# Top-k attention ahead of a mixture-of-experts attention, one core: MAX8s between the two-input instructions of the second selection level, and a re-planned order of issue

## The chip, the core and the metric

The kernel runs on one core of a Trainium2 chip. A core has engines that run side by side, each with its own in-order queue: TensorE (PE; PEld is its weight load), VectorE (DVE), ScalarE (ACT), GpSimd (POOL), and SyncE (SP), which here issues the transfers. They meet in on-chip memory and wait for each other by semaphores. The metric is the device time of one execution in microseconds, less is better. Before the change the median of 3 runs is 1224.13 us (1223.06 to 1224.57).

## The reference

Two attentions follow each other, both over 8 batches of 576 rows. The first has 8 heads of 64 and keeps for each row only the scores that are at least the row's 32nd largest:

```python
scores = scale * np.matmul(q, k.transpose(0, 1, 3, 2))
kth = np.partition(scores, -top_k, axis=-1)[..., -top_k:-top_k + 1]
scores = np.where(scores >= kth, scores, -1000000000.0)
attn = np.exp(scores - np.max(scores, axis=-1, keepdims=True))
attn = attn / (np.sum(attn, axis=-1, keepdims=True) + 1e-09)
out = np.matmul(attn, v)
```

Its output, heads side by side (512 wide), is the input of the second, which has 4 experts. Each expert is a causal attention with its own projections of 64 columns. A gate, the softmax over the two largest of 4 logits a row, weighs the experts' outputs, and each expert's result goes through its own output projection:

```python
logits = x @ w_gate                      # two largest of 4, softmax over them
for e in range(E):
    a = causal_softmax(scale * (x @ wq[e]) @ (x @ wk[e]).T)
    out += (weight of e, 0 if not chosen) * (a @ (x @ wv[e]) @ wo[e])
```

## The kernel before

**Pairs and groups.** The heads go in 32 pairs (8 batches of 4). The rows of a pair make 9 tiles of 128 rows, `j` = 0 to 8; three tiles are a group, so there are 96 groups. For each group TensorE makes the scores (`scores`, slot<-opa or opb), ScalarE copies them to memory (`copy`, L541, tile s), and VectorE selects.

**The selection on VectorE**, all of it in `topk`. `f1` (L552) takes the maxima of the two halves of each row into `fa` (3 x 288 = 864 elements a partition), `f3` (L555) the minima into `fb`. `f4` is the second level: L560 writes the maxima of the halves of `fa` into `cand`, L561 the minima back into `fa`, L563 the maxima of the halves of those maxima into `oct`, L564 their minima into `cand`; these are 432, 432, 216 and 216 elements. All six are two-input instructions (TENSOR_TENSOR). `f6` (L572) then takes the eight largest of `fb` for each of the three tiles (MAX8 over 288), `f5` those of the two halves of `fa` (72 each), and `win` and `rep` find the 32 largest in four rounds of MAX8 and MATCH_REPLACE8.

**GpSimd beside it.** `mark` (L568) is a copy of one column of `oct`. It computes nothing that is used; it makes GpSimd's queue wait until the second level is that far, and `compare` (L612, a count of candidates that could be missed) and `sub` (L454, the low half of a later pair's operands) depend on it. `tails` (L580) copies three values of `cand`.

**After the selection.** `mask` on ScalarE turns the scores and the threshold into zeros and negative numbers, `stats` makes the row's maximum and the logarithm of its sum (its transposes are `s8`, L706), `st` makes the masked scores transposed (eight products, the last of them bf16 products with the mask, 64 to 128 columns), `exp` their exponentials (pt), `av` the products with v. After four pairs `moe` runs the second attention: `vproj` and `proj` (projections), `s_stage` (scores), `t_stage` (transposes, L1035 and L1039), `c4` (transposes of scales), `avm` (products with v), `prod` (output projection). All products with matmul go through one helper, so that they have one line, L274.

**What sets the order.** No scheduler of the compiler does. The kernel's own planner (`Plan`) is given tasks, each with an engine, a cost in ns written beside it, the tasks that it waits for, the buffers that it takes, and a due time in units of pairs (the `D_...` constants and, by kind of task, the table `BIAS`). `order` then plays the engines forward: each engine takes, of the tasks that could start within `SLACK` ns of the earliest, the one that is due first. The instructions are issued in that order. `PORT` names VectorE's tasks that the planner keeps apart from GpSimd's. The order is fixed when the program is built; at run time only semaphores decide when an instruction starts.

Of the kernel before, what the change touches and what calls it, by code (L numbers as in the profile page):

```python
# [17 lines left out]
S = 576  # L18
# [46 lines left out]
class Task:  # L65
    __slots__ = ("eng", "dur", "fn", "deps", "prio", "bufs", "lat", "n", "start", "end", "outs", "left", "tag")

    def __init__(self, eng, dur, fn, deps, prio, bufs, lat):
# [27 lines left out]

class Plan:
# [8 lines left out]
    SLACK = 46.592  # L106
# [16 lines left out]
    def add(self, eng, dur, fn, deps=(), prio=0.0, bufs=(), lat=0.0, tag=None):  # L123
# [3 lines left out]
        t = Task(eng, dur, fn, [d for d in deps if d is not None], prio, bufs, lat)  # L127
        t.n, t.tag = len(self.tasks), tag
        for b in t.bufs:
            b.users += 1  # L130
            self.rings.add(b.ring)
        self.tasks.append(t)
        return t

    def order(self):
        engs = {t.eng: [0.0, []] for t in self.tasks}
        port = {"DVE": 0.0, "POOL": 0.0}
# [36 lines left out]
        out = []  # L174
        clock = Clock()
        picks, stale = {}, set(engs)
        while len(out) < len(self.tasks):
# [9 lines left out]
            dur = clock.run(s, t.dur * PEF) if e == "PE" else t.dur  # L187
# [29 lines left out]
def dve(n):  # L217
    return (n + 66) / 0.96


def pool(n):
# [5 lines left out]
BIAS = {"<lambda>": 12.025746, "again": 6.983961, "av": 0.306567, "avm": 15.637129, "c1": 5.880716, "c2": -13.131783,  # L227
        "c3": -25.554085, "c4": 3.739867, "c5": -30.11967, "cast": 21.794626, "cast_swap": -12.929197, "check1":
        -12.521071, "check2": 41.941845, "check3": -32.989098, "compare": 12.828602, "constants": -4.616309,
        "copy": -7.533133, "count": 18.029105, "diag": 13.44438, "dup": -0.254198, "dup1": -19.40904, "dup2":  # L230
# [4 lines left out]
        "load_": -6.225866, "load_swap": -1.289504, "loadv": 6.903006, "low_again": -11.353865, "m_stage":  # L235
        -39.727842, "mark": 15.671427, "mask": -11.217948, "neg": 2.920136, "neg2": -12.787457, "o_stage":
# [3 lines left out]
        "st": -0.031636, "store": -10.105639, "sub": 9.813498, "t_stage": -4.44225, "tails": 2.712787, "vproj":  # L240
        1.088363, "win": 18.27658, "xh": 2.409038, "xl": 17.765869}
D_K2 = 26.942808
D_PREP = 4.978065
D_SC = 0.540315
D_TIE = 12.261253
D_MASK = 4.158611
D_STAT = -1.038851
D_TAIL = 0.276506
D_STEP = 0.103192
D_MOE = 4.217281  # L250
D_LAST = 4.050745
D_PEN = 3.97376
D_SPAN = 4.129727
# [5 lines left out]
def kernel(ctx, tc, qk, vL, wq, wk, wv, wo, out):  # L259
# [262 lines left out]
    def topk(w, general):  # L522
# [4 lines left out]
        for g in range(3):  # L527
# [5 lines left out]
            for n, j in enumerate(js):  # L533
# [9 lines left out]
                a = add("PE", 600 if j != 4 else 1150, scores, need, bufs=[sl, s3] + used(w, j), prio=0)  # L543
# [51 lines left out]
            t = add("DVE", 2 * dve(432) + 2 * dve(216), f4, [t], bufs=[fa, c, oc], prio=P0)  # L595
            marks.append(add("POOL", 200, mark, [t], bufs=[oc], prio=-9))
            compare_last()
            t = add("DVE", 3 * dve(288), f6, [t], bufs=[fb, c], prio=P0)
            t = add("DVE", 6 * dve(72) - 45, f5, [t], bufs=[fa, c], prio=P0)
            tl = add("POOL", 200, tails, [t], bufs=[c], prio=0)  # L600
            for r in range(4):
                n = 72 if r < 2 else 168
                t = add("DVE", 3 * dve(n), lambda r=r, win=win: win(r), [t], bufs=[oc, c, w.top], prio=P0, tag="win")
                if r < 3:
                    t = add("DVE", 3 * dve(n) + 165, lambda r=r, rep=rep: rep(r), [t], bufs=[oc, c, w.top], prio=P0, tag="rep")
# [51 lines left out]
    def stats(w, x):  # L657
# [57 lines left out]
        t2 = add("POOL", 420, s2, [t], bufs=b1, prio=0)  # L715
# [6 lines left out]
        t8 = add("PE", 54 * n + 130, s8, [t2, t7], bufs=[st, sl], prio=0)  # L722
        return add("ACT", act(S) + act(64) if x == 0 else act(512), s9, [t8],
# [3 lines left out]
    def tail(w, shift, xb):  # L727
# [39 lines left out]
        for j in STO:  # L767
# [11 lines left out]
            a = add("PE", 785 if j != 4 else 1520, lambda j=j, sl=sl: st(j, sl), need, bufs=[sl, pt] + used(w, j, True) + mb, prio=2, tag="st")  # L779
# [4 lines left out]
        for j in (0, 1, 2, 3, 4):  # L784
# [3 lines left out]
            a = add("PE", 1121 if j != 4 else 833, lambda j=j, pts=pts: av(j, pts), [es[k] for k in jj] + [w.v, a],  # L788
                    bufs=pts + [acc, w.vt], prio=1, tag="av")
# [6 lines left out]
        a = add("PE", 250, neg, [c], bufs=[acc, xb], prio=1)  # L796
# [5 lines left out]
        return [c, d, add("POOL", 460, dup, [c, d], bufs=[xb], prio=1)]  # L802


    def moe(b, p, xbs, xdone, wd, span, final):
# [41 lines left out]
        for t in range(5):  # L847
# [21 lines left out]
            a = add("PE", 1440, vproj, last + wd["v"], bufs=[sl, v2] + xbs, prio=3)  # L869
# [72 lines left out]
        for gp in range(2):  # L942
# [6 lines left out]
            for name, k in (("q", 0), ("k", 2)):  # L949
# [3 lines left out]
                for dt in range(4):  # L953
# [8 lines left out]
                    a = add("PE", 800, proj, last + wd[name] + [a], bufs=[sl, qk] + xbs, prio=3)  # L962
# [11 lines left out]
                a = add("PE", 250, neg, [c], bufs=[sl, qk], prio=3, tag="neg2")  # L974
                d = add("ACT", act(S), ev2, [a], bufs=[sl, qk], prio=3)
                ready += [c, d]
                if name == "q":
# [11 lines left out]
                    spread = add("POOL", 1120, diag, [c, d], bufs=[qk, bd], prio=3)  # L989
# [3 lines left out]
            for t in (0, 1, 2, 3, 4):  # L993
# [54 lines left out]
                pe = (720, 720, 935, 1106, 920)[t]  # L1048
                when(pe)
                a = add("PE", pe, s_stage, ready + [spread], bufs=[sl, pr, sm, qk, ptm, bd], prio=3)  # L1050
# [3 lines left out]
                pe = (225, 354, 560, 800, 760)[t]  # L1054
                when(pe)
                a = add("PE", pe, t_stage, [a], bufs=[s2, pr], prio=2)
# [33 lines left out]
            a = add("POOL", 206, c1, exps, bufs=[sm], prio=3)  # L1090
# [3 lines left out]
            a = add("PE", 750, c4, [a], bufs=[sm, sl], prio=3)  # L1094
# [16 lines left out]
            a1 = add("PE", 1534, lambda av=av: av((0, 1, 2)), pts + evs, bufs=[acc, ptm, v2], prio=3, tag="avm")  # L1111
            when(1900)
            a2 = add("PE", 1750, lambda av=av: av((3, 4)), [a1], bufs=[acc, ptm, v2], prio=3, tag="avm")
# [13 lines left out]
        for t in range(5):  # L1127
# [18 lines left out]
            a = add("PE", 1470, prod, split + wd["o"], bufs=[sl, oo, o], prio=3)  # L1146
# [107 lines left out]
```

## Time and profile before

| | us |
|---|---|
| median of 3 runs | 1224.13 |
| the profiled execution | 1221.66 |
| its span, first to last instruction | 1219.9 |
| TensorE busy | 1130.6 (93%) |
| VectorE busy | 1097.2 (90%) |
| ScalarE busy | 989.3 (81%) |
| GpSimd busy | 411.2 (34%) |

The profile is one execution. Its span leaves out what lies around the first and the last instruction, which makes the execution's time a little longer. Busy time is the union of an engine's records. Records of neighbouring instructions can overlap, since an instruction's record runs from its start to the landing of its last result; the distance between two starts is then what an instruction costs its engine. For TensorE the granted clock (PEclk) is shown as a share of full speed. A row that says `<-` after a time names what ended the wait.

### The profile page before, as it was taken

To read this page: it belongs to the slowest core of one execution; us is meant where nothing else is said; L and a number is where in the kernel's file an instruction comes from. 1 tells how busy PE (TensorE), PEld (TensorE's weight loads), DVE (VectorE), ACT (ScalarE), POOL (GpSimd) and SP (SyncE) were. 2 spreads that over 40 slices of the span, in tenths; PEclk is the share of its full clock that TensorE was granted. 3 is DMA by queue.
4 is the path that set the end of the run, shared out by engine and by line. 5 is a ranking of instruction groups with operands and counts; after the bars stand their busy time and mean duration, and the time that the engine had idled before them with its cause. 6 is when DMAs were issued, how large, how long until landed. Compare 5 with 4: busy or idle time off the path is not lost. (4 is left out here: it accounts for less than half of the span.)

```text
span 1219.9 us, 28284 instructions
## 1 busy us (share of the span) xinstructions
PE 1130.6 (93%) x9330; PEld 919.9 (75%) x9330; DVE 1097.2 (90%) x4745; ACT 989.3 (81%) x2050; POOL 411.2 (34%) x803
## 2 busy tenths in 40 slices
PE   3578799999999999999999999999999999999996
PEld 3456568887788777887788877887778877887785
DVE  7999999999999999999989999899999999899021
ACT  5677777889888887989788888988888898888554
POOL 4323223424325332253224333253333442242102
PEclk8698999999999999999999999999999999999999
DMA  7132323223332232233322233323322333220101
GB/s 198 43 89 68 102 75 86 55 67 105 111 89 66 72 110 71 81 90 96 107 80 69 56 105 104 90 66 90 104 72 67 90 107 111 65 71 15 46 2 42
DMA packets 45578, 98.56 MB, mean 81 GB/s; under 512 B 7792, under 2 KB 7792, under 8 KB 45424
## 3 DMA queue, kind: packets, MB, share of 16 engines
q1 hardware_dynamic: 45424, 96.67, 28.9%
q8 instruction: 76, 1.25, 0.4%
q14 instruction: 78, 0.64, 0.2%
HBM read 32.06 MB, written 9.44 MB: 34 GB/s over the span
## 5 line engine op out<-in xcount | busy, mean ns | idle before, releaser
L781 ACT ACTIVATE pt<-slot 128x576 f32<-128x576 f32 x288 | 185.9, 652 | 101.2 <-PE slot L274 99.3
L632 ACT ACTIVATE mask<-s,top 128x576 bf16<-128x576 f32 x288 | 215.6, 773 | 8.6 <-DVE top L585 7.9
L274 PE MATMUL slot<-opa,opa 128*128 128x256 f32 (+3 forms) x984 | 200.9, 328 | 21.4 <-ACT s L541 13.6
L274 PE MATMUL acc<-pt,vt 128*64 128x320 f32 (+3 forms) x1152 | 203.3, 422 | 3.9 <-ACT pt L781 3.9
L274 PEld LDWEIGHTS slot<-opa,opa 128*128 128x128 f32 (+1 forms) x984 | 146.1, 195 | 62.1 <-ACT s L541 26.2
L274 PE MATMUL slot<-opb,opb 128*128 128x320 f32 (+1 forms) x960 | 186.1, 314 | 4.3 <-DMA opb<-raw 3.2
L541 ACT ACTIVATE s<-slot 128x576 f32<-128x576 f32 x288 | 176.1, 651 | 5.7 <-PE slot L274 5.2
L568 POOL COPY scrap<-oct 128x1 f32<-128x1 f32 x96 | 35.6, 371 | 423.0 <-DVE oct L563 422.2
L274 PEld LDWEIGHTS slot<-opb,opb 128*128 128x128 f32 x960 | 141.3, 193 | 26.0 <-issue 18.9
L585 DVE MAX8 top<-cand 128x8 f32<-128x168 f32 x576 | 152.8, 320 | 0.0
L274 PEld LDWEIGHTS acc<-pt,vt 128*64 128x64 f32 (+1 forms) x1152 | 95.0, 143 | 51.0 <-ACT pt L781 16.0
L274 PE MATMUL slot<-negi,mask 128*128 128x128 bf16 (+3 forms) x1632 | 128.4, 217 | 0.0
L552 DVE TENSOR_TENSOR fa<-s 128x864 f32<-128x864 f32 x96 | 103.7, 1081 | 21.6 <-ACT s L541 21.6
L572 DVE MAX8 cand<-fb 128x8 f32<-128x288 f32 x288 | 112.5, 446 | 0.0
L612 POOL TENSOR_TENSOR ind<-cand,top 128x513 bf16<-128x513 f32 x96 | 100.3, 1045 | 6.4 <-ACT ind L620 6.4
L555 DVE TENSOR_TENSOR fb<-s 128x864 f32<-128x864 f32 x96 | 101.0, 1052 | 0.0
L274 PEld LDWEIGHTS <-mask 128*128 128x128 bf16 (+1 forms) x1632 | 79.0, 101 | 24.3 <-issue 5.2
L585 DVE MAX8 top<-oct 128x8 f32<-128x72 f32 x576 | 94.7, 220 | 0.0
L590 DVE MATCH_REPLACE8 cand<-top,cand 128x168 f32<-128x168 f32 x288 | 88.7, 318 | 0.0
L706 PE MATMUL slot<-identf,stat 128*4 128x128 f32 x288 | 43.6, 280 | 35.4 <-DVE stat L702 23.4
L620 ACT ACTIVATE ind<-ind,tiny 128x513 bf16<-128x513 bf16 (+1 forms) x96 | 69.8, 727 | 7.2 <-POOL ind L612 6.8
L274 PE MATMUL slot<-opb,k2b 128*128 128x320 f32 x320 | 70.6, 302 | 4.2 <-ACT opb L710 3.8
(192 smaller groups left out, 2507.6 us busy)
## 6 DMA issues: line engine op xcount, KB each, us to landing
raw<-in_qk_dram SPq DMA_DIRECT2D x31, 576.0 KB, 3.7
opb<-raw SPq DMA_DIRECT2D x93, 144.0 KB, 3.4
opa<-raw SPq DMA_DIRECT2D x93, 144.0 KB, 2.4
vt<-in_vL_dram SPq DMA_DIRECT2D x32, 320.0 KB, 3.4
opb<-opb SPq DMA_DIRECT2D x62, 144.0 KB, 2.4
opa<-opa SPq DMA_DIRECT2D x62, 144.0 KB, 2.4
out_dram<-pr SPq DMA_DIRECT2D x32, 256.0 KB, 2.2
k2a<-opa SPq DMA_DIRECT2D x32, 144.0 KB, 2.3
```

Source lines behind the costliest of these rows:

```text
L274: nc.tensor.matmul(o, l, r, start=start, stop=stop, skip_group_check=True)
L541: nc.scalar.activation(s3.t[:, n], sl.t[:, o0:o0 + S], AF.Copy)
L552: v.tensor_tensor(out=fa.t, in0=s3.t[:, :, 0:288], in1=s3.t[:, :, 288:576], op=OP.max)
L555: v.tensor_tensor(out=fb.t, in0=s3.t[:, :, 0:288], in1=s3.t[:, :, 288:576], op=OP.min)
L572: v.max(out=c.t[:, n, 160:168], in_=fb.t[:, n])
L585: v.max(out=w.top.t[0][:, j, 8 * r:8 * r + 8], in_=oc.t[:, n] if r < 2 else c.t[:, n, 0:168])
L590: v.match_replace(out=c.t[:, n, 0:72] if r == 1 else src, in_values=src, imm_value=LOW, in_to_replace=w.top.t[0][:, j, 8 * r:8 * r + 8])
L612: nc.gpsimd.tensor_tensor(out=ind.t[:, 0:513].rearrange("p (a n) -> p a n", a=3), in0=c.t, in1=m32[:, js[0]:js[0] + 3, 31:32].to_broadcast ...
L620: nc.scalar.activation(ind.t[:, 0:n], ind.t[:, 0:n], AF.Sign, bias=tiny, accum_out=signs[:, 3 * w.p + g:3 * w.p + g + 1])
L632: nc.scalar.activation(w.mask[j].t, s3.t[:, n], AF.Relu, bias=w.top.t[0][:, j, 31:32], scale=-1.0)
L706: nc.tensor.transpose(sl.t[0:4, j * P:(j + 1) * P], ft(parts()[2][:, j]), identf)
L781: es[j] = add("ACT", act(S), lambda sl=sl, pt=pt, o0=o0: nc.scalar.activation(pt.t, sl.t[:, o0:o0 + S], AF.Exp, scale=0.125), [a], bufs=[s ...
```

## The change

Two things change. In the second level the three MAX8 over `fb`, which stood behind the four two-input instructions, now stand one by one between them: first, MAX8, second, MAX8, third, MAX8, fourth. `mark` now copies a column of `cand` that the fourth writes, so that it waits for the fourth instead of the third. And the planner is given another account of the engines: tasks on TensorE have a kind (LONG, SHORT, MIXED, TURN), and one that begins long behind one that ended short is charged 107 ns; their costs are written anew; GpSimd's tasks other than the mark are started at least 160 ns behind VectorE's two-input work; the tables of due times have other numbers. The order of issue of all engines comes out differently.

```diff
+LONG, SHORT, EITHER, MIXED, TURN = 1, 2, 3, 4, 5
...
-    SLACK = 46.592
+    SLACK = 48.1507
+    GAP = 160.0
+    SWITCH = 107.0
...
                 if e == "POOL":
-                    s = max(s, port["DVE"])
+                    s = max(s, port["DVE"] + (0.0 if t.tag == "mark" else self.GAP))
...
-            dur = clock.run(s, t.dur * PEF) if e == "PE" else t.dur
+            dur = t.dur
+            if t.kind:
+                if short and t.kind not in (SHORT, TURN):
+                    dur += self.SWITCH
+                t.first = short
+                short = t.kind in (SHORT, MIXED) or t.kind == EITHER and not short
+            if e == "PE":
+                dur = clock.run(s, dur * PEF)
...
-D_MASK = 4.158611
+D_MASK = 1.607309
...
-            def f4(fa=fa, c=c, oc=oc):
+            def f4(fa=fa, fb=fb, c=c, oc=oc):
+                def low(n):
+                    v.max(out=c.t[:, n, 160:168], in_=fb.t[:, n])
                 l, r = fa.t[:, :, 0:144], fa.t[:, :, 144:288]
                 v.tensor_tensor(out=c.t[:, :, 0:144], in0=l, in1=r, op=OP.max)
+                low(0)
                 v.tensor_tensor(out=l, in0=l, in1=r, op=OP.min)
+                low(1)
                 l, r = c.t[:, :, 0:72], c.t[:, :, 72:144]
                 v.tensor_tensor(out=oc.t, in0=l, in1=r, op=OP.max)
+                low(2)
                 v.tensor_tensor(out=r, in0=l, in1=r, op=OP.min)
-            def mark(oc=oc, g=g):
-                nc.gpsimd.tensor_copy(scrap[:, g:g + 1], oc.t[:, 0, 0:1])
-            def f6(fb=fb, c=c):
-                for n in range(3):
-                    v.max(out=c.t[:, n, 160:168], in_=fb.t[:, n])
+            def mark(c=c, g=g):
+                nc.gpsimd.tensor_copy(scrap[:, g:g + 1], c.t[:, 0, 143:144])
...
-            t = add("DVE", 2 * dve(432) + 2 * dve(216), f4, [t], bufs=[fa, c, oc], prio=P0)
+            t = add("DVE", 2706, f4, [t], bufs=[fa, fb, c, oc], prio=P0)
...
-            a = add("PE", 785 if j != 4 else 1520, lambda j=j, sl=sl: st(j, sl), need, bufs=[sl, pt] + used(w, j, True) + mb, prio=2, tag="st")
+            a = add("PE", 767 if j != 4 else 1500, lambda j=j, sl=sl: st(j, sl), need, bufs=[sl, pt] + used(w, j, True) + mb, prio=2, tag="st",
+                    kind=MIXED)
```

What stands in VectorE's queue for one group before, in the middle of the program (`fa`, `fb`, `cand`, `oct` as above, `s` the copied scores, `top` the values found; what stands in brackets are the semaphores that the row waits for, DVE being its own):

```order
L552 TENSOR_TENSOR fa0_89<-s31_88 128x864 [waits Activation_49]
L555 TENSOR_TENSOR fb0_90<-s31_88 128x864
L560 TENSOR_TENSOR cand1_94<-fa0_89 128x3x144 [waits DVE_49]
L561 TENSOR_TENSOR fa0_89<-fa0_89 128x3x144 [waits DVE_49]
L563 TENSOR_TENSOR oct1_92<-cand1_94 128x216
L564 TENSOR_TENSOR cand1_94<-cand1_94 128x3x72 [waits DVE_49]
L572 MAX cand1_94<-fb0_90 128x8 x3
```

And after, for a group at about the same place:

```order
L569 TENSOR_TENSOR fa0_89<-s30_87 128x864 [waits Activation_49]
L572 TENSOR_TENSOR fb0_90<-s30_87 128x864
L579 TENSOR_TENSOR cand0_93<-fa0_89 128x3x144 [waits DVE_49]
L577 MAX cand0_93<-fb0_90 128x8 [waits DVE_49]
L581 TENSOR_TENSOR fa0_89<-fa0_89 128x3x144 [waits DVE_49]
L577 MAX cand0_93<-fb0_90 128x8
L584 TENSOR_TENSOR oct0_91<-cand0_93 128x216
L577 MAX cand0_93<-fb0_90 128x8
L586 TENSOR_TENSOR cand0_93<-cand0_93 128x3x72 [waits DVE_49]
```

The three MAX8 moved into the openings; the first of them has a wait that its forerunner did not need.

On TensorE, in the second attention of the fourth batch, the two transposes of the first block of rows (`identf,pr`) and what stands around them before (`opa_1,opa_0` rows are scores, `acc<-pt,vt` is `av`, the last row begins an `st`):

```order
L274 MATMUL slot_65<-opa_1_70,opa_2_71 128x320
L274 MATMUL acc_67<-pt_122,vt_86 128x256
L274 MATMUL acc_67<-pt_122,vt_86 128x320
L274 MATMUL slot_66<-opa_1_70,opa_0_69 128x256
L274 MATMUL slot_66<-opa_1_70,opa_0_69 128x320
L274 MATMUL slot_66<-opa_1_70,opa_2_71 128x256
L274 MATMUL slot_66<-opa_1_70,opa_2_71 128x320
L1035 MATMUL slot_64<-identf,pr_145 128x128 x2
L274 MATMUL slot_65<-opa_0_75,opa_1_76 128x256
```

And after (`qk,qk` is the end of an `s_stage`, the last row begins an `st`):

```order
L291 MATMUL slot_65<-qk_3_136,qk_0_133 128x256 x2
L291 MATMUL acc_67<-pt_120,vt_86 64x256
L291 MATMUL acc_67<-pt_122,vt_86 64x256
L291 MATMUL acc_67<-pt_122,vt_86 64x320
L291 MATMUL acc_67<-pt_120,vt_86 64x320
L1053 MATMUL slot_66<-identf,pr_145 128x128 x2
L291 MATMUL slot_64<-opb_0_78,opb_1_79 128x320
```

The transposes, which stood alone between scores and masked scores, now stand directly behind an `av`, and no scores lie between.

## Rows read from the trace of the kernel before

**Rows 1.** The page: busy us, share of the span, instructions of each engine.

```profile
PE 1130.6 (93%) x9330; PEld 919.9 (75%) x9330; DVE 1097.2 (90%) x4745; ACT 989.3 (81%) x2050; POOL 411.2 (34%) x803
```

**Rows 2.** Busy us by stage: stretch, length, engines, granted clock, DMA share, GB/s.

```profile
0.00:190.00 190.00, 131.82 (x875) 100.29 (x875) 179.05 (x788) 132.54 (x247) 64.61 (x121) 0.87 0.35 96
190.00:1128.00 938.00, 919.55 (x7773) 754.16 (x7772) 903.51 (x3922) 810.71 (x1700) 330.79 (x643) 1.00 0.30 83
1128.00:1219.90 91.90, 79.19 (x686) 65.47 (x684) 14.62 (x37) 46.04 (x105) 15.81 (x40) 0.98 0.09 31
```

**Rows 3.** VectorE's waits: total us, times, longest; 190 to 1128, then 0 to 190.

```profile
DVE fa L552 <- ACT s L541: 16.9, 19, 1.6
DVE v L867 <- ACT v L864: 6.5, 17, 0.8
...
DVE fa L552 <- ACT s L541: 4.7, 2, 4.4
```

**Rows 4.** TensorE's waits from 190 to 1128, the longest in total.

```profile
PE slot L706 <- DVE top L585: 5.4, 6, 1.1
```

**Rows 5.** VectorE's timeline, one undisturbed group: start, us, instruction, count.

```profile
90.89 1.05 DVE L555 TENSOR_TENSOR fb<-s 128x864 f32<-128x864 f32 x1
91.85 0.60 DVE L560 TENSOR_TENSOR cand<-fa 128x432 f32<-128x432 f32 x1
92.49 0.61 DVE L561 TENSOR_TENSOR fa<-fa 128x432 f32<-128x432 f32 x1
93.01 0.38 DVE L563 TENSOR_TENSOR oct<-cand 128x216 f32<-128x216 f32 x1
93.42 0.38 DVE L564 TENSOR_TENSOR cand<-cand 128x216 f32<-128x216 f32 x1
93.73 1.17 DVE L572 MAX8 cand<-fb 128x8 f32<-128x288 f32 x3
94.82 0.22 DVE L576 MAX8 cand<-fa 128x8 f32<-128x72 f32 x1
```

**Rows 6.** GpSimd's groups by form: count, busy us, mean ns, idle before and releaser.

```profile
L454 POOL TENSOR_TENSOR raw<-raw,opa 128x576 f32<-128x576 f32 x31 | 51.6, 1665 | 36.6 <-ACT opa L445 36.6
L454 POOL TENSOR_TENSOR raw<-raw,opb 128x576 f32<-128x576 f32 x31 | 44.2, 1426 | 43.9 <-ACT opb L445 37.3 <-DVE top L585 4.0 <-DVE oct L590 2.6
L568 POOL COPY scrap<-oct 128x1 f32<-128x1 f32 x96 | 35.6, 371 | 423.0 <-DVE oct L563 422.2 <-DVE oct L590 0.4
```

**Rows 7.** TensorE's timeline from 610 to 622 us.

```profile
610.20 0.95 PE L274 MATMUL slot<-x,wk 128*128 128x288 f32 x6
611.08 1.19 PE L274 MATMUL acc<-pt,vt 128*64 128x256 f32 x8
...
615.59 0.96 PE L274 MATMUL slot<-x,wk 128*128 128x288 f32 x6
616.38 1.23 PE L274 MATMUL slot<-opb,opb 128*128 128x320 f32 x8
...
620.39 1.04 PE L274 MATMUL slot<-x,wk 128*128 128x288 f32 x6
621.27 1.00 PE L274 MATMUL slot<-wv,x 128*128 128x260 f32 x7
```

**Rows 8.** VectorE's first selection instruction (L552) by stage: busy us and count.

```profile
190.00:1128.00 938.00, 85.33 (x79) 1.00 0.30 83
```

**Rows 9.** Timelines of GpSimd's subtraction, twice, and of VectorE beside the first.

```profile
398.03 2.93 POOL L454 TENSOR_TENSOR raw<-raw,opa 128x576 f32<-128x576 f32 x1 [1.64 <-ACT opa L445]
...
607.42 1.40 POOL L454 TENSOR_TENSOR raw<-raw,opa 128x576 f32<-128x576 f32 x1 [3.21 <-ACT opa L445]
...
399.72 1.71 DVE L561 TENSOR_TENSOR fa<-fa 128x432 f32<-128x432 f32 x1
```

**Rows 10.** VectorE's groups by form: the second instruction of the second level, mean ns.

```profile
L561 DVE TENSOR_TENSOR fa<-fa 128x432 f32<-128x432 f32 x96 | 64.0, 666 | 3.3
```

**Rows 11.** The same instruction in the view of its tile: shortest, median, longest ns.

```profile
L561 DVE TENSOR_TENSOR fa<-fa x96: 607/608/1705, 17.7 to 1120.4; 128x432 f32<-128x432 f32 x96
```

More of the change, by code (lines that the diff above doesn't have):

```diff
@@ L65, with __init__ @@
 class Task:
-    __slots__ = ("eng", "dur", "fn", "deps", "prio", "bufs", "lat", "n", "start", "end", "outs", "left", "tag")
-    def __init__(self, eng, dur, fn, deps, prio, bufs, lat):
+    __slots__ = ("eng", "dur", "fn", "deps", "prio", "bufs", "lat", "n", "start", "end", "outs", "left", "tag", "kind",
+                 "first")
+    def __init__(self, eng, dur, fn, deps, prio, bufs, lat, kind):
+        self.kind, self.first = kind, False
         self.eng, self.dur, self.fn, self.deps = eng, dur, fn, deps
@@ L126, in add @@
         prio = self.due + prio * 1e-3 + BIAS.get(tag, 0.0)
-        t = Task(eng, dur, fn, [d for d in deps if d is not None], prio, bufs, lat)
+        t = Task(eng, dur, fn, [d for d in deps if d is not None], prio, bufs, lat, kind)
         t.n, t.tag = len(self.tasks), tag
@@ L136, in order @@
         engs = {t.eng: [0.0, []] for t in self.tasks}
-        port = {"DVE": 0.0, "POOL": 0.0}
+        port = {"DVE": -1e9, "POOL": -1e9}
+        short = False
         for t in self.tasks:
@@ L242 @@
[L242 to L245, printed above, removed]
-D_MASK = 4.158611
[L247 to L253, printed above, removed]
+BIAS = {"<lambda>": 21.16406, "again": 7.086664, "av": 0.291422, "avm": 7.96669, "c1": 6.060996, "c2": -16.917509, "c3":
+        -25.219518, "c4": 7.40449, "c5": -35.33028, "cast": 16.673692, "cast_swap": -11.231639, "check1":
+        -20.549209, "check2": 47.362819, "check3": -38.010145, "compare": 10.37121, "constants": 3.77208,
+        "copy": -5.244973, "count": 19.276636, "diag": 12.150313, "dup": -0.574571, "dup1": -16.263021, "dup2":
[4 rows of a table added]
+        "load_swap": -1.709559, "loadv": -1.18649, "low_again": -15.590234, "m_stage": -34.500069, "mark":
+        10.382567, "mask": -4.199012, "neg": 9.127403, "neg2": -15.174664, "o_stage": -15.926681, "oh":
+        -11.134218, "ol": 20.300811, "ot": -22.486721, "prod": 24.66927, "proj": 0.24706, "rep": -3.538618,
+        "s1": -38.259631, "s2": -18.732471, "s3": -11.549524, "s4": -14.828572, "s6": -6.937403, "s7": 7.577078,
+        "s8": -2.208531, "s9": -18.824699, "s_stage": 0.053481, "scores": -0.261279, "st": -0.017376, "store":
+        -19.029398, "sub": 10.142028, "t_stage": -1.573227, "tails": 9.736612, "vproj": 1.204296, "win":
+        18.47031, "xh": 7.127005, "xl": 10.21211}
@@ L254 @@
+D_K2 = 29.144853
+D_PREP = 2.849825
+D_SC = 0.543928
+D_TIE = 11.578646
+D_MASK = 1.607309
+D_STAT = -3.592427
+D_TAIL = 0.282302
+D_STEP = 0.102808
+D_MOE = 4.208214
+D_LAST = 5.999043
+D_PEN = 4.17838
+D_SPAN = 4.144087
 MP = (14,3)
@@ L542, in topk @@
                 need = w.scores[0] + w.scores[1] if j == 4 else w.scores[0 if j < 4 else 1]
-                a = add("PE", 600 if j != 4 else 1150, scores, need, bufs=[sl, s3] + used(w, j), prio=0)
+                a = add("PE", 531 if j != 4 else 1063, scores, need, bufs=[sl, s3] + used(w, j), prio=0, kind=LONG)
                 cps.append(add("ACT", act(S), copy, [a], bufs=[sl, s3], prio=0))
@@ L594, in topk @@
             t = add("DVE", dve(864), f3, cps + [t], bufs=[s3, fb], prio=P0)
-            t = add("DVE", 2 * dve(432) + 2 * dve(216), f4, [t], bufs=[fa, c, oc], prio=P0)
-            marks.append(add("POOL", 200, mark, [t], bufs=[oc], prio=-9))
+            t = add("DVE", 2706, f4, [t], bufs=[fa, fb, c, oc], prio=P0)
+            marks.append(add("POOL", 200, mark, [t], bufs=[c], prio=-9))
             compare_last()
-            t = add("DVE", 3 * dve(288), f6, [t], bufs=[fb, c], prio=P0)
             t = add("DVE", 6 * dve(72) - 45, f5, [t], bufs=[fa, c], prio=P0)
@@ L602, in topk @@
                 n = 72 if r < 2 else 168
-                t = add("DVE", 3 * dve(n), lambda r=r, win=win: win(r), [t], bufs=[oc, c, w.top], prio=P0, tag="win")
+                t = add("DVE", 3 * dve(n) - (25 if r < 2 else 0), lambda r=r, win=win: win(r), [t], bufs=[oc, c, w.top], prio=P0, tag="win")
                 if r < 3:
@@ L721, in stats @@
         t7 = add("DVE", 75, s7, [t6], bufs=b1, prio=0)
[L722 to L723 removed]
+        t8 = add("PE", 82 * n + 25, s8, [t2, t7], bufs=[st, sl], prio=0, kind=SHORT)
+        return add("ACT", 767 if x == 0 else 610, s9, [t8],
                    bufs=[st, sl] + (w.ops if x == 0 else w.ops[1:]), prio=0)
@@ L787, in tail @@
             pl.due = w.p + D_TAIL + D_STEP * (2 * j + 1.5)
-            a = add("PE", 1121 if j != 4 else 833, lambda j=j, pts=pts: av(j, pts), [es[k] for k in jj] + [w.v, a],
-                    bufs=pts + [acc, w.vt], prio=1, tag="av")
+            a = add("PE", 1020 if j != 4 else 790, lambda j=j, pts=pts: av(j, pts), [es[k] for k in jj] + [w.v, a],
+                    bufs=pts + [acc, w.vt], prio=1, tag="av", kind=SHORT)
         av_ = lambda: acc.t[:, 256:256 + S]
@@ L868, in moe @@
             when(1440)
-            a = add("PE", 1440, vproj, last + wd["v"], bufs=[sl, v2] + xbs, prio=3)
+            a = add("PE", 1436, vproj, last + wd["v"], bufs=[sl, v2] + xbs, prio=3, kind=LONG)
             e1 = add("ACT", act(256), ev, [a], bufs=[sl, v2], prio=3)
@@ L961, in moe @@
                     when(800)
-                    a = add("PE", 800, proj, last + wd[name] + [a], bufs=[sl, qk] + xbs, prio=3)
+                    a = add("PE", 795, proj, last + wd[name] + [a], bufs=[sl, qk] + xbs, prio=3, kind=LONG)
                 def ev1(sl=sl, k=k, qk=qk):
@@ L1047, in moe @@
                 n = 2 if t < 4 else 1
-                pe = (720, 720, 935, 1106, 920)[t]
+                pe = (690, 690, 923, 1095, 920)[t]
                 when(pe)
-                a = add("PE", pe, s_stage, ready + [spread], bufs=[sl, pr, sm, qk, ptm, bd], prio=3)
+                a = add("PE", pe, s_stage, ready + [spread], bufs=[sl, pr, sm, qk, ptm, bd], prio=3,
+                        kind=TURN if t < 4 else MIXED)
                 a = add("DVE", dve(n * w), m_stage, [a], bufs=[sl, sm], prio=2)
```

34 lines of the change are left out of this document (13 added, 21 removed), and 11 rows, old and new, of the table BIAS.

## Prediction, made before the change was run

> **What bounds the kernel now.** I read the page's busy shares first, then the engines by stage, then who waited for whom, and last the timelines of the second level and of some products. TensorE (93%) and VectorE (90%) are both near full, ScalarE stands at 81%; [rows 1] show no engine with room to spare but GpSimd. Three stages come out of that [rows 2]. Up to 190 us VectorE is busy 179.1 of 190 us and TensorE only 131.8: VectorE sets the pace. From 190 to 1128 us both are close to full, VectorE 903.5 and TensorE 919.6 of 938 us, at a granted clock of 1.00. After 1128 us the selection is over, and the last batch's second attention runs for 91.9 us on TensorE with VectorE at 14.6 us.
>
> The waits tell the middle stage more closely. VectorE's two largest there are 16.9 us for the copies of scores and 6.5 us for the gate's logits, and before 190 us the largest is 4.7 us [rows 3]. So VectorE hardly ever waits: whatever it is spared comes back unless another engine is late. TensorE's idle time in the middle is 938 - 919.6 = 18.4 us, 5.4 us of it in waits for the top-k values that the statistics come from [rows 4]; those move with VectorE.
>
> **Part 1: the MAX8s between the two-input instructions.** The same instructions are issued, seven a group: four TENSOR_TENSORs (432, 432, 216, 216 elements) and three MAX8s over 288. In an undisturbed group the starts are 0.64, 0.52, 0.41 and 0.31 us apart, and the three MAX8s take 94.82 - 93.73 = 1.09 us: 2.97 us in all [rows 5]. Two pairs of equal length differ in one thing. The second 432 starts 0.04 us after the first has ended (91.85 + 0.60), the third instruction starts 0.09 us before the second has ended; the fourth starts 0.03 us after the end of the third, the first MAX8 0.07 us before the end of the fourth. The late ones are those that the order shows waiting for VectorE's own semaphore, on the instruction directly ahead. So a wait on the direct predecessor costs 0.64 - 0.52 = 0.12 and 0.41 - 0.31 = 0.10 us. In the new order a MAX8 stands between each such pair. It occupies 1.09/3 = 0.36 us, longer than the 0.09 us that the predecessor still needs, so I take both waits as hidden: 2 x 0.52 + 2 x 0.31 + 1.09 = 2.75 us, 0.22 us less a group, 96 groups: 21.1 us of VectorE's time.
>
> The change adds one wait: the first MAX8 waits for the minima in fb. One 432-element instruction stands between (0.52 us), and the fb instruction ends 91.94 - 91.85 = 0.09 us after that one's start, so I price it at nothing; if it were not covered it would cost another 0.1 us a group, 9.6 us, with everything behind it on VectorE.
>
> The Trainium skill speaks against this part: "VectorE: DVE Perf Modes", section "The DRAIN you can't avoid", says that the next operation starts only when the pipe is empty, and that leaving out semaphores gains nothing. By that rule the sum of this part would be 0 instead of 21.1 us. The trace disagrees: the 0.09 and 0.07 us overlaps [rows 5] are next operations that started early. It is rival B.
>
> Part 1 moves the mark as well: GpSimd's little copy now waits for the fourth two-input instruction instead of the third. Counted from the first 432, it comes free at 2 x 0.52 + 2 x 0.31 + 3 x 0.36 + 0.07 = 2.81 us instead of 0.64 + 0.52 + 0.38 = 1.54 us. Queued behind it are the comparison, the tails' copy and the subtraction of a later pair. GpSimd stood idle 422.2 us before these 96 marks and is busy 330.8 of 938 us [rows 2, 6], so I price 1.27 us of delay at nothing. Uncovered, a repeat round would wait for the tails, at most 1.27 us a group, 79 groups, 100 us; the nearest row, that idle time, says far from it.
>
> **Part 2: the order of issue.** The number of instructions on TensorE, GpSimd and the DMA queue is the same; what moves is which piece follows which. I counted over the whole order of both kernels: a wide piece (scores, projections, output product, the masked scores) starts behind a narrow one (transposes, products into 64 columns, mask products) 438 times before and 399 now; scores, a projection or an output product is followed by a narrow piece 147 times before and 116 now. The prices come from one projection of six products: 616.38 - 615.59 = 0.79 us among wide ones, 621.27 - 620.39 = 0.88 us behind mask products, 611.08 - 610.20 = 0.88 us ahead of a narrow piece [rows 7]. That is 0.09 us for either edge: 39 x 0.09 + 31 x 0.09 = 6.3 us of TensorE's time, of which 938/1220 falls in the middle stage (4.8) and 92/1220 in the last (0.5). Bounds: 0, if the pieces that now stand side by side wait for their inputs instead, and 70 x 0.12 = 8.4 us, by the dearest hold above.
>
> The numbers for durations and due times move everything else by little; ScalarE's and the DMAs' work is unchanged. I price that at 0, with the rivals around it.
>
> **The sum.** First stage: 17 groups x 0.22 = 3.7 us, all on the path. Middle stage: 79 groups [rows 8] x 0.22 = 17.4 us if VectorE alone sets the pace; TensorE alone allows what it is spared itself, 4.8 us, and the waits for VectorE that go, 5.4 us: 10.2 us. The two have nearly the same load, so I take the middle, 13.8 us. Last stage: 0.5 us. Together 18.0 us. The profiled execution took 1221.66 us (span 1219.9); 18.0 less is 1203.7. The median of the runs before is 1224.13, 2.5 above the profiled one, so the forecast is 1206.
>
> What is late next: TensorE. With VectorE 17 us lighter in the middle stage its idle time there would have to shrink from 18.4 us to nearly nothing.
>
> **Rivals.**
> A, TensorE is the bound from 190 us on. For it: 919.6 us of records in 938. Against: its records overlap, and VectorE waits for it only a little. Then 3.7 + 4.8 + 0.5 = 9.0 us are gained: 1215.
>
> B, the two-input instruction is held all the same, the change doesn't do what it says. For it: I see no MAX8 directly ahead of a waiting two-input instruction of this level. Against: [rows 5]. TensorE's 6.3 us then lie under a VectorE as slow as before, but for the last stage: 1223.5.
>
> C, slower: GpSimd gets in at the openings. Beside the 576-element subtraction the second 432 has been seen to take 1.71 us instead of 0.61, since the subtraction, begun at 398.03, ran until 400.96; another took 1.40 [rows 9]. With a one-input MAX8 in each of three openings a waiting subtraction can slip in, and the two-input instruction behind it stands 1.40 - 0.36 = 1.04 us. There are 62 subtractions, 31 for each of two operand sets [rows 6]. The gain of 18.0 us is used up by 17 further hits; with 40 it is 41.6 - 18.0 = 23.6 us slower: 1248. Against: today's opening, the hold itself, already lets such a subtraction in, and it cost 58 ns x 96 = 5.6 us in all (mean 666 against a median of 608) [rows 10, 11]. The Trainium skill, "SBUF — State Buffer", section "SBUF: two separate sides", calls the pair of ports that both engines use an exclusive lock held for a whole instruction; [rows 9] agree.
>
> D, more than forecast: VectorE's 21.1 us come back whole, and with them the 5.6 us that the subtractions cost now, since the new waits of GpSimd keep them out: 21.1 + 5.6 + 0.5 = 27.2, so 1197.
>
> **How the numbers follow.** The forecast 0.58, A 0.20, B 0.06, C 0.08, D 0.08. This kernel's measurement can't tell 0.2% (2.4 us) from no change. The forecast, A and D are faster by more: 0.86. B lies within it: 0.06. C is slower: 0.08. The likeliest one's own range, between VectorE alone (21.6) and half-way to A, is 1202 to 1211. The range for all takes in D, with 2 us for the bounds of the order's price, and A, and goes on to where the order's 6.3 us and half of VectorE's gain are lost; it leaves out C and B: 1195 to 1221.
>
> **What would show it.** In the changed profile the second and the fourth two-input instruction should start 0.36 us after a MAX8 started, the seven together take 2.75 us; 2.97 shows B. TensorE's idle time in the middle stage should fall well under 18.4 us; if it stays while VectorE's waits grow by 10 us or more, it was A. Two-input instructions over 1 us at 432 elements, more than a handful, show C. The selection should end some 17 us before 1128 us, the stretch behind it stay near 92 us. A selection that ends earlier with a longer stretch behind it would make the sum wrong.

## The result and the profile after

The changed kernel takes 1211.66 us (1210.9 to 1215.2, 4 runs) against 1224.35 of the kernel before (its median with one run more than above): ratio 0.9903, 95% interval 0.9882 to 0.9925, 12.7 us faster. A second series gave 1210.25, ratio 0.9902 [0.9884, 0.9920]. The forecast was 1206, a gain of 18.

The page and the view by stage of the changed kernel, the columns as in [rows 1, 2]. VectorE's and ScalarE's busy times changed by less than 3 us; TensorE's fell by 5.3 us and GpSimd's by 32.8:

```profile
PE 1125.3 (93%) x9330; PEld 923.2 (76%) x9330; DVE 1096.4 (91%) x4745; ACT 986.6 (82%) x2050; POOL 378.4 (31%) x803
```

```profile
0.00:190.00 190.00, 134.82 (x888) 105.28 (x889) 177.62 (x794) 133.77 (x248) 58.93 (x119) 0.86 0.36 96
190.00:1128.00 938.00, 919.45 (x7864) 758.84 (x7863) 906.89 (x3928) 815.66 (x1719) 306.94 (x654) 1.00 0.31 83
1128.00:1209.50 81.50, 71.05 (x584) 59.10 (x579) 11.86 (x25) 37.15 (x85) 12.54 (x31) 0.98 0.09 31
```

TensorE's idle time from 190 to 1128 us has not shrunk (18.4 before, 938 - 919.45 = 18.55 now); more of the work has been done by 1128. Where the time went is read better from the starts of three groups' first instruction:

| | 1st group | 18th group | 96th group | end |
|---|---|---|---|---|
| before | 15.2 | 196.2 | 1115.8 | 1219.9 |
| after | 13.3 | 195.1 | 1105.9 | 1209.5 |

The start is 1.9 us shorter, the first 17 groups 0.8 us longer (181.0 to 181.8), the 78 groups of the middle 8.8 us shorter (919.6 to 910.8), the rest 0.5. In the profile of the second series the first 17 groups took 179.7 us and the middle 910.4, so the sign of the 0.8 means nothing. The four add to 10.4 us, the difference of the two profiled executions; the medians differ by 12.7, since the profiled execution before lay 2.7 us under its median and the one after only 0.4.

VectorE's timeline of a group of the changed kernel in which nothing interferes (start, duration, instruction), which answers to [rows 5]:

```profile
88.69 0.59 DVE L579 TENSOR_TENSOR cand<-fa 128x432 f32<-128x432 f32 x1
89.21 0.45 DVE L577 MAX8 cand<-fb 128x8 f32<-128x288 f32 x1
89.58 0.58 DVE L581 TENSOR_TENSOR fa<-fa 128x432 f32<-128x432 f32 x1
90.08 0.45 DVE L577 MAX8 cand<-fb 128x8 f32<-128x288 f32 x1
90.45 0.36 DVE L584 TENSOR_TENSOR oct<-cand 128x216 f32<-128x216 f32 x1
90.74 0.45 DVE L577 MAX8 cand<-fb 128x8 f32<-128x288 f32 x1
91.11 0.36 DVE L586 TENSOR_TENSOR cand<-cand 128x216 f32<-128x216 f32 x1
91.39 0.22 DVE L594 MAX8 cand<-fa 128x8 f32<-128x72 f32 x1
```

91.39 - 88.69 = 2.70 us instead of 2.97. Over all 96 groups the mean, without waits for other engines, fell from 3.06 to 2.77 us: 0.28 us a group, 27.1 us of VectorE's time. Yet VectorE is as busy as before: other instructions got longer. The last two-input instruction of the statistics (`s7`, L719, before L702) does 5 or 4 elements a partition. The timelines of VectorE and of GpSimd in the changed kernel:

```profile
287.39 0.75 DVE L1133 TENSOR_TENSOR ot<-slot,sm 128x576 f32<-128x576 f32 x1
288.06 1.42 DVE L719 TENSOR_TENSOR stat<-stat,stat 128x4 fp32r<-128x4 f32 x1
289.39 0.22 DVE L594 MAX8 cand<-fa 128x8 f32<-128x72 f32 x1
```

```profile
288.03 1.42 POOL L471 TENSOR_TENSOR raw<-raw,opa 128x576 f32<-128x576 f32 x1
```

An instruction of 0.15 us takes 1.42 us, the time of the subtraction that began 0.03 us before it. In the view of its line (shortest, median, longest ns) before and after:

```profile
L702 DVE TENSOR_TENSOR stat<-stat,stat x64: 146/154/341, 45.5 to 1135.1; 128x5 fp32r<-128x5 f32 x32, 128x4 fp32r<-128x4 f32 x32
```

```profile
L719 DVE TENSOR_TENSOR stat<-stat,stat x64: 154/167/1429, 39.6 to 1122.2; 128x5 fp32r<-128x5 f32 x32, 128x4 fp32r<-128x4 f32 x32
```

I summed over the trace what VectorE's two-input instructions take above the shortest tenth of their line and form where GpSimd works beside them (differences over 60 ns), and call it *stretch*. Before it is 11.1 us (5.5 at the second 432, 3.0 at the first selection instruction); after it is 25.9: 11.7 at `s7`, 5.1 at the statistics' first instruction `s1` (L689), 5.9 at the first 432 behind GpSimd's work on the second attention.

VectorE's waits and TensorE's longest from 190 to 1128 us, which answer to [rows 3, 4]:

```profile
DVE fa L569 <- ACT s L558: 11.2, 8, 1.7
DVE v L885 <- ACT v L882: 4.5, 10, 0.6
```

```profile
PE slot L723 <- DVE stat L719: 10.0, 13, 0.8
```

VectorE waits less for others than before (16.9 and 6.5), and TensorE's longest wait is now for the stretched instruction.

### The profile page after: what moved, and what is told of

It is laid out like the page before. It is cut to its first block, busy times and chain, and to the rows that moved or that the text cites. A ratio compares the mean times of both kernels' runs of the same rounds, so it can differ in the third digit from the quotient of the medians.

```text
span 1209.5 us, 28181 instructions
## 1 busy us (share of the span) xinstructions
PE 1125.3 (93%) x9330; PEld 923.2 (76%) x9330; DVE 1096.4 (91%) x4745; ACT 986.6 (82%) x2050; POOL 378.4 (31%) x803
## 5 line engine op out<-in xcount | busy, mean ns | idle before, releaser
L649 ACT ACTIVATE mask<-s,top 128x576 bf16<-128x576 f32 x288 | 216.4, 772 | 10.6 <-DVE top L603 10.0
L291 PE MATMUL slot<-opa,opa 128*128 128x256 f32 (+3 forms) x984 | 196.1, 326 | 25.1 <-ACT s L558 15.3
L291 PE MATMUL acc<-pt,vt 128*64 128x256 f32 (+3 forms) x1152 | 199.6, 423 | 1.9 <-ACT pt L799 1.9
L590 POOL COPY scrap<-cand 128x1 f32<-128x1 f32 x96 | 18.1, 189 | 534.9 <-DVE cand L586 528.3
L577 DVE MAX8 cand<-fb 128x8 f32<-128x288 f32 x288 | 130.4, 453 | 0.0
L291 PE MATMUL slot<-opa,k2a 128*128 128x256 f32 (+1 forms) x320 | 70.1, 301 | 1.5 <-ACT opa L727 1.5
```

The costliest lines, as they stand in the source:

```text
L291: nc.tensor.matmul(o, l, r, start=start, stop=stop, skip_group_check=True)
L649: nc.scalar.activation(w.mask[j].t, s3.t[:, n], AF.Relu, bias=w.top.t[0][:, j, 31:32], scale=-1.0)
```

## The experiments

All times are medians; each ratio is to the kernel before on the same chip, and is formed from all runs, so that it can differ by 0.1% from the quotient of two medians. Where an order is said to be kept, it is kept on every engine.

**Part 1 alone, in the old order.**

```diff
 (before)  f4, mark and f6 as in the change; tasks, costs, due times and order as before
-mark: copies oct, written by the third two-input instruction
+mark: copies cand, written by the fourth
```

> The order of issue of before, instruction for instruction on TensorE, ScalarE, GpSimd and SyncE, with only the three MAX8s put between the two-input instructions and the mark on the fourth. Theory V (VectorE is on the path; the whole change's 26 us of spared VectorE time was half eaten by about 15 us of new waits of the statistics' two-input instructions behind GpSimd, which the new order brought): here few such waits, so 14 to 20 us faster than before, 1204 to 1210. Theory T (TensorE is the bound from 190 us on, its lighter order brought the gain): 4 to 6 us faster, 1218 to 1220.

Measured 1233.73 us, ratio 1.0098 [1.0083, 1.0113]: 10.6 us slower. The second level is lighter all the same. What is late shows on VectorE before (first fence) and in this kernel (second), at the same place of the order:

```profile
776.37 0.60 DVE L560 TENSOR_TENSOR cand<-fa 128x432 f32<-128x432 f32 x1
...
778.24 0.68 DVE L1015 TENSOR_REDUCE sm<-slot 128x2 f32<-128x512 f32 x1
778.84 0.15 DVE L867 COPY v<-slot 128x4 f32<-128x4 f32 x1
```

```profile
780.31 0.60 DVE L561 TENSOR_TENSOR cand<-fa 128x432 f32<-128x432 f32 x1
...
783.02 0.68 DVE L1017 TENSOR_REDUCE sm<-slot 128x2 f32<-128x512 f32 x1
783.62 0.22 DVE L869 COPY v<-slot 128x4 f32<-128x4 f32 x2
```

The copy of the gate's logits starts 3.31 us after the first 432 instead of 2.47, since in the old order it stood ahead of the three MAX8s and now stands behind all seven. TensorE's timeline there, and its wait from 190 to 1128 us:

```profile
782.67 0.43 PE L274 MATMUL acc<-x,negr 128*128 128x256 f32 x2
783.82 1.33 PE L274 MATMUL slot<-opa,opa 128*128 128x256 f32 x8 [0.72 <-DVE v L869]
```

```profile
PE acc L274 <- ACT pt L783: 7.3, 10, 1.0
PE slot L274 <- DVE v L869: 6.3, 14, 0.8
```

Before, the second of these waits was 0.2 us, and the first, for ScalarE's exponentials, 2.3; VectorE's wait for TensorE's scores of the second attention grew too, from 3.1 to 11.5 us. These two were not followed to their source. In 58 of the 96 groups of the old order pieces like that copy (reductions, copies of logits, products for the second attention) stand between the fourth two-input instruction and the MAX8s.

**The order alone.** The mark stays on the fourth two-input instruction.

```diff
 (after)   mark and order kept
-TT, MAX8, TT, MAX8, TT, MAX8, TT
+TT, TT, TT, TT, MAX8, MAX8, MAX8
```

> The order of issue of the changed kernel on every engine, with the seven instructions of the second level in their old sequence (four two-input ones, then three MAX8s). Theory V: VectorE has its 0.26 us a group back and keeps the new waits behind GpSimd, so slower than the changed kernel by 15 to 25 us, 1227 to 1237, no faster than before. Theory T: 3 to 6 us slower than the changed kernel, 1215 to 1218.

Measured 1221.45 us, 0.9985 [0.9972, 0.9998]: 1.6 us faster. TensorE's busy time is 1124.1 us, 6.5 below before, but the stretch is 27.3 us, and the line of `s7` in this kernel reads

```profile
L718 DVE TENSOR_TENSOR stat<-stat,stat x64: 151/257/1029, 40.4 to 1130.7; 128x5 fp32r<-128x5 f32 x32, 128x4 fp32r<-128x4 f32 x32
```

So this stretch needs no openings between the instructions; it is there with the new order alone. The MAX8s between the instructions are worth some 10 us inside the new order (1221.45 - 1211.66 = 9.8, or 0.9985 - 0.9903 by the ratios); in the old one, with the mark moved, they cost 10.6.

**The statistics' instruction without its two inputs from SBUF (the on-chip memory).** Its first input goes through unused columns of the accumulator's tile in PSUM, the memory that TensorE writes to, in the changed kernel and, as a control, in the one before.

```diff
-activation(z[:, 1], z[:, 0], AF.Ln, bias=eps)
+activation(ACC.tiles[0][:, 960 + 8 * x:960 + 8 * x + n], z[:, 0], AF.Ln, bias=eps)
```

> The changed kernel, order untouched; the second logarithm of the statistics is written to the accumulator memory (unused columns) instead of on-chip memory, so that the tiny subtraction of 4 or 5 elements (L719 in the changed kernel) has one input there and one here. Theory V: its stretches of 0.4 to 1.2 us behind GpSimd, 10.8 us in all, go; 5 to 10 us faster than the changed kernel, 1202 to 1207. Theory T, or a port that such an instruction needs all the same: no change, 1211 to 1213.

> Control: the same edit on the kernel before, where that subtraction was stretched by 0.36 us in all. Both theories: no change, 1223 to 1226. If it is faster by more than 3 us, the edit does something else than taking the subtraction away from GpSimd's port.

Measured 1211.32, 0.9909 [0.9895, 0.9924], and 1231.45, 1.0071 [1.0057, 1.0086]. In the changed kernel the edit takes all 11.7 us of stretch at `s7` away, and the time stays. But the control costs 8 us where there was nothing to take away, so the edit brings waits of its own: TensorE now waits for ScalarE's write into the tile that it accumulates in (first line, the changed kernel with the edit), VectorE for TensorE in the control (second line). The pair decides nothing.

```profile
PE acc L291 <- ACT acc L715: 5.7, 13, 0.6
DVE stat L702 <- PE acc L274: 4.3, 7, 1.3
```

**Part 1 only where nothing stands between, mark on the third.**

```diff
 (before)  order kept
+for x, y in zip(row, row[1:]):
+    if x.tag == "f4" and y.tag == "f6": x.fn.mix[0] = True    # 38 groups
```

> The order of before on every engine; the MAX8s go between the two-input instructions only in the 38 of 96 groups in which nothing else stood between the fourth two-input instruction and the three MAX8s in VectorE's queue; mark on the third as before. Theory Q (in the old order, all 96 interleaved were 10.6 us slower because 58 urgent instructions, such as reduces and the copies that free a PSUM slot, then stand behind 1.1 us of MAX8s): the loss goes, 0 to 8 us faster than before, 1215 to 1223. Theory P (the loss came from GpSimd entering at the openings or from the later mark): the loss shrinks only in proportion, 38/96 of it, 3 to 5 us slower than before.

**Part 1 alone with the mark on the third in all groups.**

> All 96 groups interleaved in the old order, but GpSimd's mark on the third two-input instruction as before. Theory Q: as slow as with the mark on the fourth, 1231 to 1236. Theory P with the later mark as its cause: the loss goes, 1210 to 1223. Theory P with GpSimd's entering as its cause: slower still, over 1236, since it is let in earlier.

Measured 1229.78, 1.0060 [1.0041, 1.0079], and 1272.33, 1.0389 [1.0371, 1.0406]. The mark lets GpSimd go on, and its comparison gets in at the opening ahead of the fourth instruction. VectorE and GpSimd of the second kernel:

```profile
605.74 0.44 DVE L559 MAX8 cand<-fb 128x8 f32<-128x288 f32 x1
606.11 1.19 DVE L568 TENSOR_TENSOR cand<-cand 128x216 f32<-128x216 f32 x1
607.22 0.23 DVE L578 MAX8 cand<-fa 128x8 f32<-128x72 f32 x1
```

```profile
605.88 0.19 POOL L571 COPY scrap<-oct 128x1 f32<-128x1 f32 x1 [4.50 <-DVE oct L566]
606.02 1.05 POOL L614 TENSOR_TENSOR ind<-cand,top 128x513 bf16<-128x513 f32 x1
```

The view of that line with the mark on the third, then on the fourth (part 1 alone, above):

```profile
L568 DVE TENSOR_TENSOR cand<-cand x96: 356/1193/1551, 19.8 to 1169.8; 128x216 f32<-128x216 f32 x96
```

```profile
L568 DVE TENSOR_TENSOR cand<-cand x96: 353/364/2218, 19.7 to 1131.4; 128x216 f32<-128x216 f32 x96
```

0.84 us at the median, 59.8 us of stretch at this instruction in all, and some 37 us of time (47.9 us slower than the kernel before in the same series, instead of 10.6). In the 38 groups of the first of the two it was 21.2 us of stretch.

**Less work for TensorE, less for VectorE.** The changed kernel, without two of the six products of each output block; and with MAX8 over 192 of the 288 minima, which leaves out part of the candidates.

```diff
-for x, w in ((0, 0), (2, 0), (0, 1)):
+for x, w in ((0, 0), (2, 0)):
```

```diff
-v.max(out=c.t[:, n, 160:168], in_=fb.t[:, n])
+v.max(out=c.t[:, n, 160:168], in_=fb.t[:, n, 0:192])
```

> The changed kernel without two of the six products of each output projection (the low part of the weights; about 0.46 us in each of 40, 18 us of TensorE's work). Theory T (TensorE is the bound from 190 us on): 12 to 18 us faster than the changed kernel, 1194 to 1200. Theory V (VectorE is): 0 to 5 us faster.

> The changed kernel with the three MAX8s over 192 instead of 288 of the minima (a third of the candidates of this kind is not looked at), 0.10 us each, 29 us of VectorE's work. Theory V: 15 to 25 us faster than the changed kernel, 1187 to 1197. Theory T: 0 to 6 us faster, 1206 to 1212.

Measured 1207.89, 0.9869 [0.9851, 0.9887], and 1202.17, 0.9816 [0.9800, 0.9832]: 3.8 and 9.5 us below the changed kernel; the first is hardly clear of the noise. TensorE's busy time fell by 10.2 us (to 1115.1), by 7.1 of them in the 78 middle groups (893.2 to 886.1), but these took 910.0 us instead of 910.8; most of the gain (2.7 us) lies behind the start of the last group. The lighter MAX8s took 23.4 us off VectorE in the middle, which shortened by 9.9 us (to 900.9). So in the middle VectorE sets the pace and TensorE hardly; a good half of what VectorE is spared does not come back as time, and its waits grow. With the lighter VectorE (190 to 1128 us):

```profile
DVE fa L569 <- ACT s L558: 12.5, 10, 1.7
DVE v L885 <- ACT v L882: 8.2, 14, 1.4
DVE sm L1033 <- PE slot L291: 6.1, 18, 0.5
DVE stat L719 <- ACT stat L715: 4.4, 13, 1.3
```

**GpSimd kept behind the statistics.**

```diff
 (after)   order kept
+s7.seen = lambda: ft(parts()[2][:, 0, 3:4])
...
+if t.eng == "DVE" and t.tag in pl.PORT:
+    seen = getattr(t.fn, "seen", None)
+if t.eng == "POOL" and t.tag in ("sub", "compare") and seen is not None:
+    nc.gpsimd.tensor_copy(scrap2[:, 0:1], seen())    # 41 copies
+    seen = None
```

> The changed kernel, with one small GpSimd copy ahead of the subtraction or comparison that follows the statistics' last two-input instruction (s7) in the planned order; the copy reads that instruction's result, so that GpSimd can no longer get in ahead of it. The order on the other engines is unchanged. In the changed kernel these statistics' instructions stood 10.8 us behind GpSimd in all. Theory 'the new stretches ate the gain': the 10.8 us go, and at 0.2 to 0.33 us of time per us of VectorE the kernel is 2 to 4 us faster than the changed one, 1207.5 to 1210. Rival 'the stretches lie beside other waits': 10.8 us go from the trace and come back as waits of VectorE for other engines, 1210.5 to 1212.5. Rival 'the copies hold GpSimd up, and the minima behind them come late': slower, 1213 to 1220.

> The changed kernel once more, as the baseline of the two others on the same chip: 1211 to 1212.5 by every theory, ratio 0.990 to the kernel before.

Measured 1204.32, 0.9848 [0.9831, 0.9865], beside 1210.25, 0.9902 [0.9884, 0.9920], of the changed kernel: 5.9 us faster, the fastest of the kernels that leave nothing out, and more than expected. The same place as at 288.06 above, VectorE and GpSimd:

```profile
287.84 0.15 DVE L720 TENSOR_TENSOR stat<-stat,stat 128x4 fp32r<-128x4 f32 x1
287.91 0.23 DVE L595 MAX8 cand<-fa 128x8 f32<-128x72 f32 x1
```

```profile
288.06 0.19 POOL L1221 COPY scrap<-stat 128x1 f32<-128x1 f32 x1 [0.20 <-DVE stat L720]
288.26 1.42 POOL L472 TENSOR_TENSOR raw<-raw,opa 128x576 f32<-128x576 f32 x1
```

The subtraction comes 0.23 us later, and 1.27 us are saved. The stretch at `s7` is 1.7 us instead of 11.7; the middle stage takes 904.8 us instead of 910.8. TensorE's wait for `s7` there falls from 10.0 us to

```profile
PE slot L725 <- DVE stat L720: 5.6, 8, 0.8
```

**Is it the later mark or the urgent pieces that made part 1 alone slow?** Two tests: the 38 free groups with the mark on the fourth; and part 1 alone with 47 such copies, ahead of GpSimd's comparisons and subtractions, that read what the gate's comparison (`g1`) and `s7` wrote.

```diff
 (38 groups, order kept)
-nc.gpsimd.tensor_copy(scrap[:, g:g + 1], oc.t[:, 0, 0:1])
+nc.gpsimd.tensor_copy(scrap[:, g:g + 1], c.t[:, 0, 143:144] if mix[0] else oc.t[:, 0, 0:1])
```

```diff
 (part 1 alone)
+g1.seen = lambda: gg.t[2][:, 0, 0, 0:1]    # 6 copies, and 41 behind s7 as above
...                                          # a comparison issued just ahead of g1 or s7 goes behind it;
                                             # every engine's own order is kept
```

> The kernel before in its old order, MAX8s between the two-input instructions only in the 38 groups in which nothing stood between the fourth two-input instruction and the first MAX8; the mark waits for the fourth there. No urgent instruction is moved behind the block. Theory 'part 1 alone lost because 58 urgent instructions fell behind the MAX8s': without them it gains, at most 38 x 0.22 = 8.4 us of VectorE, a third to all of it in the time: 1215 to 1221, against 1223 before. Rival 'the later mark is what cost': 38/96 of the loss of 10.6 us stay, about 4 us slower: 1226 to 1229.

> Part 1 alone in the old order (96 groups interleaved, mark on the fourth instruction, 1233.7 us in its own run, +10.6 us to the kernel before), with 47 small GpSimd copies ahead of comparisons and subtractions, which read what the gate's comparison (6) or the statistics' last two-input instruction (41) has written; the order on the other engines is unchanged. In part 1 alone GpSimd's work, held longer by the later mark, had come to lie beside these: 5.1 us of stretch at the gate, 4.2 us at the statistics, of 19.2 us in all (11.1 in the kernel before). Theory 'about half of the loss is GpSimd moved beside two-input instructions by the later mark': at some 0.55 us of time per us of stretch 9.3 us less make it 5 us faster, 1227 to 1230, ratio about 1.005. Rival 'the loss is VectorE's urgent instructions that stand behind the MAX8s alone': the stretches go, the time stays at 1231 to 1235, ratio about 1.01. If the copies hold GpSimd's later work up: above 1235.

Measured 1224.93, 1.0020 [1.0007, 1.0033], and 1235.12, 1.0100 [1.0079, 1.0122]. The first lies between both expectations: moving the mark in these groups makes 1229.78 into 1224.93, but no gain is left. With the 58 groups as they were, TensorE's wait for the copy of logits (6.3 us with part 1 alone) is gone, and the loss falls from 10.6 to 2.1 us:

```profile
PE slot L274 <- DVE v L874: 0.2, 1, 0.2
```

The second is the rival's: the gate's instruction, longer with part 1 alone (first fence), is as short as it ever was with the copies (second), and the time stays.

```profile
L883 DVE TENSOR_TENSOR g<-v x8: 233/1080/1084, 230.0 to 1201.0; 128x80 bf16<-128x80 f32 x8
```

```profile
L885 DVE TENSOR_TENSOR g<-v x8: 232/232/235, 230.4 to 1201.5; 128x80 bf16<-128x80 f32 x8
```

TensorE's wait for the copy of logits stays too (6.1 us, 14 times). The copies did less than expected, though: the stretch fell from 19.2 to 15.2 us, at `s7` only from 4.2 to 3.3, so the test bears on the gate alone. Both tests speak for the urgent pieces as the cause of most of the 10.6 us; neither shows it by itself, since the first also takes the 58 groups' MAX8s out from between the instructions. Why the 38 free groups gain nothing is open: the gate is stretched there as well (5.2 us), and the last test says that this costs little.

## Why the prediction was right, and which terms were mis-sized

The direction and the range held (1195 to 1221); the gain was 12.7 us instead of 18.0. The path through VectorE was right. What VectorE saved was more than forecast, and a loss that the forecast did not have took more than the excess; that the range held in spite of both is partly luck.

*The 0.22 us a group* was right in kind and a little small. A MAX8 that stands where VectorE had waited for its own last result starts 0.52, 0.50 or 0.29 us behind its forerunner, and the next two-input instruction 0.37 us later (predicted: 0.36). The seven take 2.70 us, not 2.75; the gain is 0.27 us in an undisturbed group and 0.28 over all groups, 27.1 us instead of 21.1. The wait of the first MAX8 for the minima costs nothing, as priced. Rival B is out. The prediction read the Trainium skill, "VectorE: DVE Perf Modes", section "The DRAIN you can't avoid", as speaking against this part, and took only half of it: the section says that leaving out semaphores gains nothing, but also that a next operation that is not held starts earlier. The 0.27 us disagree with the first; the second agrees with the rows above, in which each MAX8 starts 0.07 or 0.08 us before the end of the instruction ahead.

*The mark, priced at nothing*, costs the changed kernel one wait of 0.6 us (a repeat round for the copy that marks) and one of 0.3 (for the tails behind it), but its place decides: on the third instruction it lets in GpSimd's comparison, 0.84 us at the median and some 37 us of time in all. So rival C's mechanism is real, with a comparison at the fourth instruction in place of a subtraction at the second, and near its price (1.04 us a hit); the moved mark keeps it away. The 7 first 432s over 1 us in the changed kernel (1.44 us) are not C's either: no MAX8 stands ahead of them, and they are as long with the order alone. The Trainium skill, "SBUF — State Buffer", section "SBUF: two separate sides", calls the ports an exclusive lock for a whole instruction; 1.42 us beside 1.42 us agrees.

*The 6.3 us of TensorE* were right as work: its busy time fell by 5.3 us, and by 6.5 with the order alone.

*"The numbers for durations and due times move everything else by little; ... I price that at 0"* is the step that failed. The new order puts GpSimd's subtractions, comparisons and products of the second attention beside the statistics and the first 432: 25.9 us of stretch instead of 11.1, 14.8 us of VectorE's time, and TensorE waits for the statistics. Taking 10 us of it away at `s7` gave back 5.9 us of time, about the 5.3 that are missing from the sum; that the two agree so closely is in part chance, as the other terms below were off as well.

*The middle stage, 13.8 us*, measured 8.8. "What is late next: TensorE" was wrong, and rival A with it: its idle time did not shrink, and 7.1 us less of its work there shortened the middle by 0.8. The mean of the two bounds was too high, and what held the gain down was not TensorE: VectorE's second level, 21.2 us shorter in the middle, lost 13.3 of it to `s1` and `s7` (start to next start, the sums before and after: 33.7 to 47.0), which leaves 7.9 of the 8.8. The 96th group began 9.9 us sooner, not 17.

*The first stage, 3.7 us "all on the path"*, gave next to nothing (181.0 us before; 181.8 and 179.7 after): its second level is 7.6 us shorter from start to start (0.9 us of that was a wait for another engine), but VectorE then waits, 2.8 us of it for scores at one place, and is stretched at the statistics; even the MAX8s over 192 left that stage at 181.1 us. What came is 1.9 us at the start, not foreseen. *The last stage's 0.5 us* came.

*That the two parts' gains add* was taken for granted and is wrong. The order alone changes the time by -1.6 us, part 1 alone by +10.6, both by -12.7. In the changed kernel 71 of 96 groups have another piece right behind the seven, and TensorE never waits for the copy of logits: the planner was given the block's length (2706 ns) and laid its readers accordingly. That this length by itself does it was not tried.

## What to carry to other kernels

Independent instructions between dependent ones filled the waits here, 0.27 us a group, but the block that grew together made what stood behind it later, and in the old order the kernel lost by it. So change the schedule with it, and test each part alone as well as both. A change of order has to be read for what it lays side by side on engines that share a port: look for short two-input instructions whose longest time is that of a GpSimd instruction. And a tiny copy that reads what must come first, put ahead of the long GpSimd instruction, is a cheap way to settle who goes first: 41 of them were worth 5.9 us here, 47 in the old order nothing.

## What had not been expected of the hardware

A two-input instruction of 0.15 us took up to 1.43 us when GpSimd's 1.42 us subtraction began 0.03 us ahead of it, while one-input MAX8s kept theirs: in the changed kernel those over 168 elements have a median of 319 ns, both the 109 that lie wholly beside a two-input GpSimd instruction and the 379 that touch none. And a us of VectorE has not one price: of 10.6 us spared at `s7` (start to next start) the middle stage got 6.0 back, of 23.4 us in the MAX8s 9.9, of 5.1 us at the gate, in the old order, nothing.
